# LSH attention before two feed-forward layers on one Trainium2 core: a pair's preparation takes all of the queries, then all of the keys

## Chip, cores and metric

One core of a Trainium2 chip runs the whole program. The metric is the device time of one execution in microseconds. A measurement is several executions; their median is compared.

## What is computed

For 2 batches of 8 heads, 768 positions and 64 dimensions, attention is masked by hash buckets: six sign bits of a projection give each query and each key a bucket, and only pairs in the same bucket count. Two feed-forward layers follow; they have no part in the change.

```python
q_bits = (np.einsum('bhsd,dk->bhsk', q, proj) > 0)
k_bits = (np.einsum('bhsd,dk->bhsk', k, proj) > 0)
mask = q_bucket[:, :, :, None] == k_bucket[:, :, None, :]
scores = np.where(mask, scale * q @ k.T, -1e9)
attn = softmax(scores)              # with + 1e-9 in the denominator
x = (attn @ v) as 1536 x 512
h = x @ w_in;  x = (h * cos(h)) @ w_out
out = (silu(x @ w_gate) * (x @ w_val)) @ w_out2
```

## The kernel before, in words

**Pairs and steps.** The 16 heads are taken as eight pairs. A pair is six steps of 128 query rows (steps 0 to 5; the code's `u` counts 48 of them, `i = u % 6`). `att_step` (L569) writes out the order of a step by hand: scores of head 0 (`mm_scores`, L421), transposes of the probabilities of two steps ago, the AV matmuls (`av`, L485) for a half pair finished before, scores of head 1, more transposes. VectorE takes the row maxima out of PSUM (L438), ScalarE the exponentials (L449), GpSimd multiplies by the reciprocal sums (the norms, L460, two to a step). Every engine works through its own queue in program order, and so does SP, which issues all transfers.

**Operands of the scores.** fp32 products are made of rounded high parts and low parts. For a pair of heads, `mm_scores` adds two matmuls in PSUM: X by Y (L429) and Z by W (L431). X holds the queries' high part in its first 64 rows and their low part in the others; Y holds the keys' high part twice; Z holds the queries' high part and, in 12 rows more, sign bits of the queries; W holds the keys' low part and sign bits of the keys. Each of the four has two buffers, so that one pair's are filled while the pair before is computed. The first scores of a pair (step 0) need all of the four.

**Preparation of a pair.** `prep(pr)` (L231) is a generator that is advanced at four places of every step (`fill`, L565), 24 times in a pair, while the pair before is computed. For pairs from 2 on it goes in this order:

- calls 1 and 3 (step 0): queries of head 0 and 1 are transposed on TensorE (L243), scaled and copied to `raw["q"]` (in the rows "qT") by ScalarE (L249);
- calls 5 and 7 (step 1): VectorE rounds the queries to `hi["q"]` ("qH", L257); the keys are transposed and copied to `raw["k"]` ("kT") by VectorE (L253);
- call 9 (step 2): VectorE rounds the keys ("kH"); SP is given eight copies of 192 KB, for each half X, Z, Y and Y (L260 to L263); TensorE projects (L285), VectorE makes the bits in a tile `bt` (L289), GpSimd scales them (L293), and SP is given eight transfers of bits, four to Z and four to W (L308);
- call 11 (step 2): GpSimd subtracts, `raw["q"] - hi["q"]`, in place (L314), and SP is given two transfers of it to X (L320);
- call 13 (step 3): the same for the keys, to W.

Since SP works in order and each transfer waits for its data, a transfer that waits holds all behind it. Pair 1 has the same parts with other places for bits and other counts of calls, within steps of pair 0; pair 0 is prepared by `prep_first` without transfers.

**What else SP issues.** Queries and keys of the pair after next are loaded at step 4 (`load_pair`, L213; "qn" and "kn"), values at step 5 ("vn"), and a weight block of 512 KB at steps 2 and 5 from u = 5 to u = 32 (`fetch_next`, L96, issues at L106 or L110). Three steps after its load a weight is rebuilt: one copy by ScalarE (L125) and three operations by VectorE (L140, L144, L148), spread over the fills of a step (steps 2 and 5 from u = 8 to u = 35).

**Small tiles.** The pool `sm` (L203) has eight buffers each of row minima (`mn`), sums (`sv`) and reciprocals (`rv`).

Of the kernel before, what the change touches and what calls it, by code (L numbers as in the profile page):

```python
# [10 lines left out]
F32 = mybir.dt.float32  # L11
# [3 lines left out]
ALU = mybir.AluOpType  # L15
PSUM = bass.MemoryType.PSUM

P = 128
# [8 lines left out]
def lsh_attention_moe_moe2(  # L27
# [13 lines left out]
    nc = tc.nc  # L41
# [158 lines left out]
    ld = actx.enter_context(tc.tile_pool(name="ld", bufs=1))  # L200
    pre = actx.enter_context(tc.tile_pool(name="pre", bufs=1))
    pp = actx.enter_context(tc.tile_pool(name="pp", bufs=6))
    sm = actx.enter_context(tc.tile_pool(name="sm", bufs=8))  # L203

    pj0 = {nm: pre.tile([P, D], F32, tag="pj0" + nm, name="pj0" + nm) for nm in "qk"}
    pjs = pre.tile([P, NB], F32, tag="pjs", name="pjs")
# [4 lines left out]
    heads = {}  # L211
# [15 lines left out]
    def prep_psum(pr, i, name):  # L227
        pool, tag = (ps_v, "av") if pr == 1 and i % 2 else (ps_p, "pp")
        return pool.tile([P, 512], F32, tag=tag, name=name)

    def prep(pr):  # L231
# [4 lines left out]
        X, Y, Z, W = (  # L236
            qk.tile([P, 2, S], F32R, tag=nm, bufs=2, name=f"{nm}{pr}") for nm in "XYZW"
        )
        for nm in ("q", "k"):
            for j in range(2):  # L240
                ps = prep_psum(pr, j, f"tr{nm}{pr}_{j}")
                for c in range(HB):
                    nc.tensor.transpose(  # L243
                        ps[:, c * P : (c + 1) * P],
                        nat[nm, pr][:, j, 2 * c : 2 * c + 2, :].rearrange("p c d -> p (c d)"),
                        ident,
                    )
                if nm == "q" or pr == 1:
                    nc.scalar.activation(  # L249
                        out=raw[nm][:, j, :], in_=ps[:, :HALF], func=AF.Copy, scale=TAKEN[nm]  # L250
                    )
                else:
                    nc.vector.tensor_copy(raw[nm][:, j, :], ps[:, :HALF])  # L253
                yield
                if pr > 1:
                    yield
            nc.vector.tensor_copy(hi[nm], raw[nm])  # L257
        for e in range(2):
            r, cs = slice(e * D, (e + 1) * D), slice(e * HALF, (e + 1) * HALF)
            nc.sync.dma_start(out=X[:D, :, cs].bitcast(F32), in_=hi["q"][r].bitcast(F32))  # L260
            nc.sync.dma_start(out=Z[:D, :, cs].bitcast(F32), in_=hi["q"][r].bitcast(F32))
            nc.sync.dma_start(out=Y[:D, :, cs].bitcast(F32), in_=hi["k"][r].bitcast(F32))
            nc.sync.dma_start(out=Y[D:, :, cs].bitcast(F32), in_=hi["k"][r].bitcast(F32))  # L263


        if pr == 1:
            bt = early.tile([P, 2, DM], F32, tag="raw", bufs=2, name="bt1")[:, :, :HALF]
            for j in range(2):
                ps = prep_psum(pr, j, f"pj1_{j}")
                for g, nm in enumerate(("q", "k")):  # L270
                    nc.tensor.matmul(
                        out=ps[g * D : (g + 1) * D, :HALF], lhsT=pj0[nm], rhs=raw[nm][:, j, :],
                        start=True, stop=True,
                    )
                nc.vector.tensor_scalar(
                    out=bt[:, j], in0=ps[:, :HALF], scalar1=0.0, scalar2=cvec[:, 1:2],
                    op0=ALU.is_gt, op1=ALU.subtract,
                )
        else:
            bt = pre.tile([P, HALF], F32, tag="bt", name=f"bt{pr}")  # L280
            ps = prep_psum(pr, 4, f"pj{pr}")
            for g, nm in enumerate(("q", "k")):
                for j in range(2):
                    r0 = 32 * (2 * g + j)
                    nc.tensor.matmul(  # L285
                        out=ps[r0 : r0 + 32, :HALF], lhsT=pj[nm], rhs=raw[nm][:, j, :],
                        start=True, stop=True,
                    )
            nc.vector.tensor_scalar(  # L289
                out=bt, in0=ps[:, :HALF], scalar1=0.0, scalar2=cvec[:, 0:1],  # L290
                op0=ALU.is_gt, op1=ALU.subtract,
            )
# [3 lines left out]
        for g, dst in enumerate((Z, W)):  # L296
            rows = slice(D, D + 2 * NB)
            for e in range(2):
                cs = slice(e * HALF, (e + 1) * HALF)
                if pr == 1:  # L300
                    r0 = D * g + 32 * e
                    nc.sync.dma_start(
                        out=dst[rows, :, cs].bitcast(F32), in_=bt[r0 : r0 + 2 * NB]
                    )
                    continue
                for j in range(2):
                    r0 = 32 * (2 * g + j) + 2 * NB * e
                    nc.sync.dma_start(  # L308
                        out=dst[rows, j, cs].bitcast(F32), in_=bt[r0 : r0 + 2 * NB]
                    )  # L310
        yield
        yield
        for nm in ("q", "k"):
            nc.gpsimd.tensor_tensor(  # L314
                out=raw[nm], in0=raw[nm], in1=hi[nm].bitcast(F32), op=ALU.subtract
            )
            for e in range(2):
                cs = slice(e * HALF, (e + 1) * HALF)
                dst = X[D:, :, cs] if nm == "q" else W[:D, :, cs]
                nc.sync.dma_start(out=dst.bitcast(F32), in_=raw[nm][e * D : (e + 1) * D])  # L320
            yield
            yield
        heads[pr] = (X, Y, Z, W)

    def prep_first():

# [20 lines left out]
                    )  # L347
            return ps

        def lows(eng, dst, j, nm, hi, e):  # L350
            r, cs = halves[e]
            eng.tensor_tensor(  # L352
                out=dst[:, j, cs], in0=raw[nm][r, j, :], in1=hi[:, j, cs].bitcast(F32),
                op=ALU.subtract,
            )

        ps = transposes(0)
        for j in range(2):
            for nm in ("q", "k"):
                nc.scalar.activation(  # L360
                    out=raw[nm][:, j, :], in_=ps[nm][:, :HALF], func=AF.Copy, scale=TAKEN[nm]
                )
            pb = ps_p.tile([P, 512], F32, tag="pp", name=f"pj0_{j}")
            for g, nm in enumerate(("q", "k")):
                nc.tensor.matmul(
                    out=pb[g * D : (g + 1) * D, :HALF], lhsT=pj0[nm], rhs=raw[nm][:, j, :],
                    start=True, stop=True,
                )
            if j == 0:
                ps = transposes(1)  # L370
            for dst, nm, es in ((Y, "k", (0, 1)), (X, "q", (0,))):
                for e in es:
                    r, cs = halves[e]
                    if j or nm == "k":
# [11 lines left out]
            lows(nc.gpsimd, W[:D], j, "k", Y[:D], 0)  # L386
            lows(nc.vector, X[D:], j, "q", X[:D], 0)
            nc.vector.tensor_scalar(
                out=bt[:, j, :], in0=pb[:, :HALF], scalar1=0.0, scalar2=cvec[:, 1:2],
                op0=ALU.is_gt, op1=ALU.subtract,  # L390
            )
            for e in range(2):
                cs = halves[e][1]
                src, dst = bt[D + 32 * e : D + 32 * e + 2 * NB, j], W[D : D + 2 * NB, j, cs]
                if e:
                    nc.gpsimd.tensor_scalar(
                        out=dst, in0=src, scalar1=-BIG, scalar2=1.0, op0=ALU.mult, op1=ALU.mult
                    )
                else:
                    nc.scalar.activation(out=dst, in_=src, func=AF.Copy, scale=-BIG)  # L400
            lows(nc.vector, W[:D], j, "k", Y[:D], 1)
            nc.vector.tensor_copy(Z[D : D + 2 * NB, j, :HALF], bt[: 2 * NB, j])
            yield
        for j in range(2):
# [7 lines left out]
            lows(nc.vector, X[D:], j, "q", X[:D], 1)  # L412
            yield

    scores = {}
# [469 lines left out]
```

## Time and profile before

| | |
|---|---|
| three runs | 819.39, 820.34, 823.87 us; median 820.34 |
| the profiled execution | 822.72 us, of which the span from the first to the last instruction is 820.9 |
| busy, share of the span | TensorE 97%, weight loads 76%, VectorE 57%, ScalarE 61%, GpSimd 55% |
| attention | from the start to about 265 us |
| feed-forward layers | from there to the end |
| issues on SP's queue, in the attention | copies of high parts, bits and low parts, loads of q, k, v, ten weight blocks |

How to read it: TensorE's busy time is modelled from pipelined matmuls, so a share near 100% says that it was fed, not that it was at its peak. What a stall is worth is read better from the distance between the same instructions of successive steps. The attention has a rhythm of six steps, and its stretches are compared with one another.

In the rows, PE is TensorE, PEld its weight loads, DVE VectorE, ACT ScalarE, POOL GpSimd, SPq the queue of SP.

### The profile page before, as it was taken

Reading aid. Unit: us, or ns where it says so; the run is one execution under the profiler, and the core shown is the slowest. Engines: PE = TensorE matmul, PEld = TensorE weight load, DVE = VectorE, ACT = ScalarE, POOL = GpSimd, SP = SyncE. Lnnn points to the kernel's source line nnn. Section 1 sums busy time; section 2 is a strip of 40 time slices with the busy share of each in tenths; the row PEclk is TensorE's granted clock in tenths of the full one; section 3 lists DMA queues with packets and bytes.
Section 4 is the critical chain, followed back from the end, with each engine's and each line's share of the span. In section 5 each row is a group of like instructions: output and inputs, shape, how many; then the busy total and the mean of one; then the engine's idle time right before and its main releaser. Section 6 shows DMA issues by size and latency. Waiting matters only on the chain.

```text
span 820.9 us, 11429 instructions
## 1 busy us (share of the span) xinstructions
PE 795.2 (97%) x3956; PEld 622.6 (76%) x3956; DVE 466.5 (57%) x865; ACT 499.6 (61%) x941; POOL 454.1 (55%) x394
## 2 busy tenths in 40 slices
PE   6899999998999999999999999999999999999998
PEld 4666666666675788888888888888888888888886
DVE  5888987887673999987755688752122111121112
ACT  5777767766685888887767777743334333343332
POOL 4754553653562677677776767744444444445440
PEclk8999999999999999999999999999999999999999
DMA  3745645644502455433220234300001000010001
GB/s 115 179 115 171 168 128 169 172 124 118 149 1 78 129 160 175 154 103 102 79 76 1 63 120 128 101 0 1 1 0 53 1 1 0 1 52 0 1 1 51
DMA packets 47049, 66.52 MB, mean 81 GB/s; under 512 B 3824, under 2 KB 41872, under 8 KB 46992
## 3 DMA queue, kind: packets, MB, share of 16 engines
q1 hardware_dynamic: 46992, 65.80, 27.4%
q8 instruction: 31, 0.51, 0.3%
q14 instruction: 26, 0.21, 0.1%
HBM read 45.09 MB, written 3.15 MB: 59 GB/s over the span
## 4 chain that ended last, share of the span: by engine, by line
PE 86%; DVE 6%; DMA 3%; issue 1%; POOL 1%; ACT 1%; SPq 1%; POOLq 0%; DVEq 0%; ACTq 0%
PE o L608 9%; PE o L610 9%; PE o L609 9%; PE av L491 6%; PE h L608 5%; PE h L610 5%; PE h L609 5%; PE t L473 5%; PE gate L609 4%; PE val L609 4%; PE val L608 4%; PE gate L608 4%; PE gate L610 4%; PE val L610 4%; PE s L429 3%; PE s L431 3%
## 5 line engine op out<-in xcount | busy, mean ns | idle before, releaser
L460 POOL TENSOR_SCALAR p<-p,rv 128x768 f32<-128x768 f32 x96 | 89.4, 942 | 106.3 <-DVE rv L457 99.2
L783 DVE TENSOR_TENSOR u<-val,sg 128x512 f32<-128x512 f32 x36 | 24.9, 692 | 198.7 <-ACT sg L777 188.4
L438 DVE TENSOR_SCALAR_CACHE_REDUCE p<-s 128x768 f32<-128x768 f32 x96 | 91.7, 955 | 46.7 <-PE s L431 38.4
L479 ACT ACTIVATE pt<-t 128x384 f32<-128x384 f32 x144 | 66.9, 486 | 53.6 <-PE t L473 53.5
L449 ACT ACTIVATE p<-p,mn 128x768 f32<-128x768 f32 x96 | 89.6, 934 | 9.4 <-DVE p L438 9.2
L473 PE MATMUL t<-ident,p 128*128 128x128 f32 x576 | 86.2, 274 | 6.0 <-DVE pt L481 5.6
L473 PEld LDWEIGHTS t<-ident,p 128*128 128x128 f32 x576 | 67.4, 140 | 17.1 <-DVE pt L481 7.5
L491 PE MATMUL av<-pt,vn 128*64 128x384 f32 x384 | 72.1, 498 | 0.0
L429 PE MATMUL s<-Y,X 128*128 128x512 f32 x192 | 59.2, 390 | 1.8 <-DVE X L352 1.8
L431 PE MATMUL s<-W,Z 76*128 76x512 f32 x192 | 51.2, 348 | 8.7 <-issue 3.8
L642 ACT ACTIVATE r<-r 128x512 f32<-128x512 f32 x48 | 30.4, 633 | 41.8 <-DVE r L634 41.8
L630 DVE SCALAR_TENSOR_TENSOR rf<-ki,h 128x512 f32<-128x512 int32 x46 | 32.0, 695 | 35.9 <-ACT ki L627 35.6
L429 PEld LDWEIGHTS s<-Y,X 128*128 128x128 f32 x192 | 29.3, 193 | 28.8 <-DVE pt L481 8.4
L125 ACT ACTIVATE w<-raw 128x512 f32<-128x512 f32 x68 | 44.6, 659 | 0.0
L491 PEld LDWEIGHTS av<-pt,vn 128*64 128x64 f32 x384 | 23.4, 136 | 25.8 <-issue 25.8
L654 DVE TENSOR_TENSOR g<-h,r 128x512 f32<-128x512 f32 x48 | 33.1, 689 | 16.9 <-ACT r L643 16.6
L431 PEld LDWEIGHTS s<-W,Z 76*128 76x128 f32 x192 | 30.3, 194 | 15.1 <-issue 7.9
L144 DVE SCALAR_TENSOR_TENSOR bw<-w,bw 128x512 int32<-128x512 int32 x55 | 38.0, 691 | 1.2
L140 DVE TENSOR_SCALAR bw<-raw 128x512 int32<-128x512 int32 x55 | 38.0, 691 | 1.0
L148 DVE SCALAR_TENSOR_TENSOR w<-raw,bw 128x512 int32<-128x512 int32 x55 | 37.5, 683 | 0.9
L643 ACT ACTIVATE r<-r,halfpi 128x512 f32<-128x512 f32 x48 | 34.8, 724 | 1.6
L627 ACT ACTIVATE ki<-h 128x512 int32<-128x512 f32 x48 | 28.3, 590 | 11.2 <-PE h L610 11.2
(1872 smaller groups left out, 2298.7 us busy)
## 6 DMA issues: line engine op xcount, KB each, us to landing
raw<-in_moe_w_out_dram SPq DMA_DIRECT2D x28, 512.0 KB
raw<-in_moe_w_in_dram SPq DMA_DIRECT2D x16, 512.0 KB
raw<-in_moe_w_gate_dram SPq DMA_DIRECT2D x12, 512.0 KB
raw<-in_moe_w_val_dram SPq DMA_DIRECT2D x12, 512.0 KB
Y<-kH SPq DMA_DIRECT2D x28, 192.0 KB
vn<-in_v_dram SPq DMA_DIRECT2D x8, 384.0 KB
out_dram<-ot SPq DMA_DIRECT2D x12, 256.0 KB
qn<-in_q_dram SPq DMA_DIRECT2D x7, 384.0 KB
```

The costliest lines, as they stand in the source:

```text
L125: nc.scalar.activation(out=t, in_=raws[i][:, :, 1].bitcast(F32), func=AF.Copy, scale=2.0**-112)
L429: nc.tensor.matmul(out=ps[:, ks], lhsT=X[:, j, qs], rhs=Y[:, j, ks], start=True, stop=False)
L431: nc.tensor.matmul(out=ps[:, ks], lhsT=Z[:KZ, j, qs], rhs=W[:KZ, j, ks], start=False, stop=True)
L438: nc.vector.tensor_scalar(out=pt, in0=ps[:, :S], scalar1=-MASKED, scalar2=None, op0=ALU.min, op1=ALU.min, accum_out=mn,)
L449: nc.scalar.activation(out=pt, in_=pt, func=AF.Exp, bias=nbias.pop((u, j)), scale=-1.0, accum_out=sums[u][:, j : j + 1],)
L460: nc.gpsimd.tensor_scalar(out=pt, in0=pt, scalar1=rv[:, j : j + 1], scalar2=1.0, op0=ALU.mult, op1=ALU.mult)
L473: nc.tensor.transpose(ps[:, c * P : (c + 1) * P], src[:, kb * P : (kb + 1) * P], ident)
L479: nc.scalar.activation(out=o, in_=s3, func=AF.Copy)
L491: nc.tensor.matmul(out=ps[j * D : (j + 1) * D, :HALF], lhsT=nat["v", pr][:, j, BLOCKS[kb], :], rhs=pts[half, j][:, kb, :], start=(kb == 0) ...
L608: nc.tensor.matmul(out=out_ap, lhsT=sh, rhs=mh, start=first, stop=False)
L609: nc.tensor.matmul(out=out_ap, lhsT=sh, rhs=ml, start=False, stop=False)
L610: nc.tensor.matmul(out=out_ap, lhsT=sl, rhs=mh, start=False, stop=last)
```

## The change

The preparation of a pair from 2 on takes all that belongs to the queries before the keys. X and Z are filled right after the queries are rounded (call 5), both halves of X, then both of Z; GpSimd makes the queries' low part in the same call and SP is given its two transfers. The low part goes to a tile of its own ("low"), since the transposed queries are still needed for the projection. After the projection the first half of the queries' tile takes the bits; the tile `bt` is gone. Y is filled in call 9, both halves of one copy, then of the other; bits and their transfers follow as before. The keys' low part comes in call 11, and the generator ends two calls earlier. For pair 1 only the order of the eight copies changes. `sm` has four buffers instead of eight. The helper of the same name in `prep_first` is renamed. The list `heads[pr]` is set at the beginning.

```diff
-    sm = actx.enter_context(tc.tile_pool(name="sm", bufs=8))
+    sm = actx.enter_context(tc.tile_pool(name="sm", bufs=4))
...
             nc.vector.tensor_copy(hi[nm], raw[nm])
-        for e in range(2):
-            r, cs = slice(e * D, (e + 1) * D), slice(e * HALF, (e + 1) * HALF)
-            nc.sync.dma_start(out=X[:D, :, cs].bitcast(F32), in_=hi["q"][r].bitcast(F32))
-            nc.sync.dma_start(out=Z[:D, :, cs].bitcast(F32), in_=hi["q"][r].bitcast(F32))
-            nc.sync.dma_start(out=Y[:D, :, cs].bitcast(F32), in_=hi["k"][r].bitcast(F32))
-            nc.sync.dma_start(out=Y[D:, :, cs].bitcast(F32), in_=hi["k"][r].bitcast(F32))
+            for dst in (X[:D], Z[:D]) if nm == "q" else (Y[:D], Y[D:]):
+                for e in range(2):
+                    r, cs = slice(e * D, (e + 1) * D), slice(e * HALF, (e + 1) * HALF)
+                    nc.sync.dma_start(
+                        out=dst[:, :, cs].bitcast(F32), in_=hi[nm][r].bitcast(F32)
+                    )
+            if pr > 1 and nm == "q":
+                lows(pr, nm, raw, hi)
...
-            bt = pre.tile([P, HALF], F32, tag="bt", name=f"bt{pr}")
...
+            bt = raw["q"][:, 0, :]
             nc.vector.tensor_scalar(
                 out=bt, in0=ps[:, :HALF], scalar1=0.0, scalar2=cvec[:, 0:1],
...
+        bits(pr, bt)
         yield
         yield
-        for nm in ("q", "k"):
-            nc.gpsimd.tensor_tensor(
-                out=raw[nm], in0=raw[nm], in1=hi[nm].bitcast(F32), op=ALU.subtract
-            )
...
+        for nm in ("q", "k") if pr == 1 else ("k",):
+            lows(pr, nm, raw, hi)
             yield
             yield
...
+    def lows(pr, nm, raw, hi):
+
+        X, _, _, W = heads[pr]
+        t = raw[nm]
+        if pr > 1 and nm == "q":
+            t = pre.tile([P, 2, HALF], F32, tag="low", name=f"{nm}L{pr}")
+        nc.gpsimd.tensor_tensor(out=t, in0=raw[nm], in1=hi[nm].bitcast(F32), op=ALU.subtract)
+        for e in range(2):
+            cs = slice(e * HALF, (e + 1) * HALF)
+            dst = X[D:, :, cs] if nm == "q" else W[:D, :, cs]
+            nc.sync.dma_start(out=dst.bitcast(F32), in_=t[e * D : (e + 1) * D])
```

`bits` is the block of eight transfers of L296 to L310 as a function, word for word.

## Rows read from the trace of the kernel before

**Rows 1.** Attention: length, busy PE, PEld, DVE, ACT, POOL, then PEclk, DMA share, GB/s.

```profile
20.00:265.00 245.00, 231.26 (x1481) 158.22 (x1482) 184.32 (x411) 175.01 (x383) 125.91 (x124) 1.00 0.49 132
```

**Rows 2.** The same view, from one step's first AV matmul to the next step's.

```profile
36.81:41.52 4.71, 4.71 (x33) 3.40 (x32) 2.97 (x8) 3.49 (x10) 1.79 (x2) 1.00 0.94 296
112.38:116.74 4.36, 4.36 (x29) 3.07 (x28) 4.08 (x7) 2.59 (x6) 4.31 (x4) 1.00 0.58 140
116.74:121.68 4.94, 4.60 (x30) 3.05 (x29) 4.30 (x10) 3.25 (x9) 2.33 (x4) 1.00 0.62 130
65.86:71.72 5.86, 5.14 (x32) 3.36 (x31) 5.39 (x14) 4.50 (x12) 1.96 (x2) 1.00 0.97 275
96.02:101.75 5.73, 5.15 (x33) 3.37 (x33) 5.29 (x13) 4.58 (x12) 1.95 (x2) 1.00 0.98 283
126.04:132.39 6.35, 4.93 (x32) 3.38 (x32) 5.18 (x11) 4.52 (x12) 1.96 (x2) 1.00 0.98 286
156.68:163.07 6.39, 5.15 (x33) 3.36 (x32) 5.60 (x14) 4.56 (x12) 2.02 (x3) 1.00 0.96 272
187.36:194.66 7.30, 4.92 (x33) 3.38 (x32) 5.18 (x11) 4.44 (x12) 1.96 (x2) 1.00 0.94 252
218.40:224.13 5.73, 4.60 (x30) 3.06 (x29) 2.63 (x8) 3.57 (x10) 1.78 (x2) 1.00 0.94 251
```

**Rows 3.** TensorE in order of time at two pair ends: start, duration, instruction, idle.

```profile
130.89 0.59 PE L431 MATMUL s<-W,Z 76*128 76x512 f32 x2 [1.42 <-issue]
...
162.27 0.55 PE L243 MATMUL trq<-ident,qn 128*128 128x128 f32 x3 [0.49 <-DMA qn<-in_q_dram]
```

**Rows 4.** The chain of work that ended last, at the end of pair 3.

```profile
125.26 4.58 DMA W<-kT
```

**Rows 5.** SP's queue in order of time, preparation of pair 4.

```profile
107.85 0.60 SPq L260 DMA_DIRECT2D X<-qH  x1
...
112.74 0.59 SPq L262 DMA_DIRECT2D Y<-kH  x1
...
114.68 0.73 SPq L261 DMA_DIRECT2D Z<-qH  x1
...
116.36 0.95 SPq L263 DMA_DIRECT2D Y<-kH  x1
117.41 3.23 SPq L308 DMA_DIRECT2D Z<-bt  x4
120.69 2.99 SPq L308 DMA_DIRECT2D W<-bt  x4
123.79 1.37 SPq L320 DMA_DIRECT2D X<-qT  x2
125.26 1.25 SPq L320 DMA_DIRECT2D W<-kT  x2
...
131.27 0.34 SPq L106 DMA_DIRECT2D raw<-in_moe_w_out_dram  x1
```

**Rows 6.** Busy time by engine, steps 2 to 4 of pair 3; DMA share and GB/s last.

```profile
114.00:120.00 6.00, 5.66 (x37) 4.04 (x38) 5.65 (x11) 3.09 (x7) 3.39 (x4) 1.00 0.90 202
120.00:125.00 5.00, 5.00 (x34) 3.65 (x34) 4.39 (x9) 4.24 (x12) 4.58 (x5) 1.00 0.10 22
```

**Rows 7.** GpSimd in order of time, steps 1 to 3 of pair 3.

```profile
107.41 2.03 POOL L460 TENSOR_SCALAR p<-p,rv 128x768 f32<-128x768 f32 x2 [3.42 <-DVE rv L457]
...
115.06 1.82 POOL L314 TENSOR_TENSOR qT<-qT,qH 128x768 f32<-128x768 f32 x1
...
121.25 1.83 POOL L314 TENSOR_TENSOR kT<-kT,kH 128x768 f32<-128x768 f32 x1
```

**Rows 8.** VectorE in order of time, step 2 of pair 3.

```profile
112.63 0.61 DVE L289 TENSOR_SCALAR bt<-pj,cvec 128x384 f32<-128x384 f32 x1
...
115.81 1.63 DVE L144 SCALAR_TENSOR_TENSOR w<-w,raw 128x512 int32<-128x512 int32 x1
117.47 0.69 DVE L148 SCALAR_TENSOR_TENSOR w<-raw,w 128x512 int32<-128x512 int32 x1
```

More of the change, by code (lines that the diff above doesn't have):

```diff
@@ L229, in prep_psum, with bits @@
         return pool.tile([P, 512], F32, tag=tag, name=name)
+    def bits(pr, bt):
+        _, _, Z, W = heads[pr]
+        rows = slice(D, D + 2 * NB)
+        for g, dst in enumerate((Z, W)):
+            for e in range(2):
+                cs = slice(e * HALF, (e + 1) * HALF)
+                if pr == 1:
+                    r0 = D * g + 32 * e
+                    nc.sync.dma_start(
+                        out=dst[rows, :, cs].bitcast(F32), in_=bt[r0 : r0 + 2 * NB]
+                    )
+                    continue
+                for j in range(2):
+                    r0 = 32 * (2 * g + j) + 2 * NB * e
+                    nc.sync.dma_start(
+                        out=dst[rows, j, cs].bitcast(F32), in_=bt[r0 : r0 + 2 * NB]
+                    )
     def prep(pr):
@@ L235, in prep @@
             hi[nm] = pre.tile([P, 2, HALF], F32R, tag=nm + "H", name=f"{nm}H{pr}")
-        X, Y, Z, W = (
+        X, Y, Z, W = heads[pr] = [
             qk.tile([P, 2, S], F32R, tag=nm, bufs=2, name=f"{nm}{pr}") for nm in "XYZW"
-        )
+        ]
         for nm in ("q", "k"):
@@ L257, in prep @@
             nc.vector.tensor_copy(hi[nm], raw[nm])
[L258 to L263 removed]
+            for dst in (X[:D], Z[:D]) if nm == "q" else (Y[:D], Y[D:]):
+                for e in range(2):
+                    r, cs = slice(e * D, (e + 1) * D), slice(e * HALF, (e + 1) * HALF)
+                    nc.sync.dma_start(
+                        out=dst[:, :, cs].bitcast(F32), in_=hi[nm][r].bitcast(F32)
+                    )
+            if pr > 1 and nm == "q":
+                lows(pr, nm, raw, hi)
         if pr == 1:
@@ L295, in prep @@
         )
[L296 to L310, printed above, removed]
+        bits(pr, bt)
         yield
         yield
-        for nm in ("q", "k"):
-            nc.gpsimd.tensor_tensor(
-                out=raw[nm], in0=raw[nm], in1=hi[nm].bitcast(F32), op=ALU.subtract
[L316 to L320, printed above, removed]
+        for nm in ("q", "k") if pr == 1 else ("k",):
+            lows(pr, nm, raw, hi)
             yield
             yield
-        heads[pr] = (X, Y, Z, W)
+    def lows(pr, nm, raw, hi):
[4 more added lines that the diff above has]
+        nc.gpsimd.tensor_tensor(out=t, in0=raw[nm], in1=hi[nm].bitcast(F32), op=ALU.subtract)
+        for e in range(2):
+            cs = slice(e * HALF, (e + 1) * HALF)
+            dst = X[D:, :, cs] if nm == "q" else W[:D, :, cs]
+            nc.sync.dma_start(out=dst.bitcast(F32), in_=t[e * D : (e + 1) * D])
     def prep_first():
@@ L348, in transposes, with rest_of @@
             return ps
-        def lows(eng, dst, j, nm, hi, e):
+        def rest_of(eng, dst, j, nm, hi, e):
             r, cs = halves[e]
@@ L385, in prep_first @@
             yield
-            lows(nc.gpsimd, W[:D], j, "k", Y[:D], 0)
-            lows(nc.vector, X[D:], j, "q", X[:D], 0)
+            rest_of(nc.gpsimd, W[:D], j, "k", Y[:D], 0)
+            rest_of(nc.vector, X[D:], j, "q", X[:D], 0)
             nc.vector.tensor_scalar(
@@ L400, in prep_first @@
                     nc.scalar.activation(out=dst, in_=src, func=AF.Copy, scale=-BIG)
-            lows(nc.vector, W[:D], j, "k", Y[:D], 1)
+            rest_of(nc.vector, W[:D], j, "k", Y[:D], 1)
             nc.vector.tensor_copy(Z[D : D + 2 * NB, j, :HALF], bt[: 2 * NB, j])
@@ L411, in prep_first @@
             )
-            lows(nc.vector, X[D:], j, "q", X[:D], 1)
+            rest_of(nc.vector, X[D:], j, "q", X[:D], 1)
             yield
```

## The prediction

> **What bounds the kernel now.** I read the stretches first: in the attention part TensorE is busy 231.26 of 245.00 us, so some 14 us are open there [rows 1]; in the two feed-forward parts behind it TensorE is not idle, and nothing of this change lies there. So the question is what TensorE waits for in the attention.
>
> Then I cut the attention at the starts of the AV matmuls, one such group to a step. A step without preparation work takes 4.36 us with TensorE busy throughout; a step that also has one of the four transposes of the next pair's preparation takes 4.71 [rows 2]. Against this stands the stretch over a pair's end, from the AV of step 5 to the AV of the next pair's step 0. With one query transpose in it, it should take 4.71, and does so from pair 0 to pair 1 (the 4.71 row is that one; it builds no weight). From pair 1 on it takes 5.86, 5.73, 6.35, 6.39, 7.30 and, where nothing is left to prepare, 5.73 against 4.36 [rows 2]. The excess is 1.15 + 1.02 + 1.64 + 1.68 + 2.59 + 1.37 = **9.45 us**.
>
> What is waited for: the first scores of the new pair. The matmul of W and Z starts at 130.89 after 1.42 us of idle, so it could have started at 129.47; at other pair ends the query transpose behind it waits for qn, the load of the pair after next, as at 162.27 [rows 3]. The profile puts the first wait down to "issue", but the chain of work names the real end: a transfer of kT to W that runs from 125.26 for 4.58 us [rows 4].
>
> Why is that transfer issued so late? GpSimd had the low part of the keys at 121.25 + 1.83 = 123.08 [rows 7], but the SP queue got to it at 125.26. SP issues one transfer after the other from 112.74 to 126.51: six of the eight copies of high parts (X and Z of the first half had gone out at 107.85), eight of sign bits (3.23 + 2.99 us), two of the queries' low part (1.37), two of the keys' (1.25), and only behind them qn [rows 5]. Meanwhile the DMA engines were nearly empty: 0.10 of their time from 120 to 125, against 0.90 at 202 GB/s before [rows 6]. At a pair's end the limit is the issue order on one queue.
>
> **The change, part by part.**
>
> Queries first. Of the 20 preparation transfers of a pair from 2 on, two (X and Z of the second half) now follow the first two at 107.85 instead of standing among those of the keys, and the two of the queries' low part follow as soon as GpSimd has made it. They take some 0.60 (as the X at 107.85), 0.73 and 1.37 us, so 2.70 with their gaps about 3.0 us of SP's time that leaves the crowded stretch [rows 5].
>
> When will those be issued? GpSimd does the low part right behind its two norms of step 1, which end at 107.41 + 2.03 = 109.44; with 1.82 for the subtraction it is ready at 111.27 [rows 7]. X, X, Z, Z go from 107.85 to about 110.5, the two low transfers from 111.3 to 112.7. One weight load that SP issued ahead of the queries (the kind at 131.27, 0.34 us) now stands behind them, since SP first waits for the queries of step 1. So Y's four start near 113.1 instead of 112.74: this gives back 0.4 us.
>
> Does SP then go faster? In the old burst the issues grew from 0.59 to 0.95 us [rows 5]. A copy of 192 KB at 202 GB/s is 0.97 us, by which I read 0.95 as SP paced by the engines. The new order puts more behind Y early on (six copies and a weight load), so I let Y take 0.60 to 0.95 each, 3.6 in all with gaps, and the bits 6.5 to 6.9 (they took 6.27 from the first to the end of the last). The keys' low part then goes out near 123.6, at best 122.2, at worst 124.4 (Y at 0.95 and the first group of bits drawn out likewise), instead of 125.26: 0.9 to 3.1 us earlier. I take 1.65. It gains again on arrival: the queries' 384 KB, at 202 GB/s 1.9 us, no longer stand ahead of it in the engines, of which I count 1.3. That makes about 3 us, estimates from the rows named, against losses of 1.02 to 2.59. The qn load moves with it, by 1.65 at least, and its waits were shorter than that. I expect the six stretches at 4.71 and 4.36 but for some 0.4 us at the largest and 0.15 us here and there: **gain 8.9 us**. The bounds are 0.9 per pair end, 6 x 0.9 = 5.4, and the whole 9.45.
>
> The Trainium skill, "DMA: Bandwidth & Descriptors", section Bandwidth, has copies within SBUF bound by the fabric at 435 GB/s; by that a 192 KB copy is 0.45 us (an estimate), SP would never be paced, and the gain were the full 9.45. The row's 202 GB/s with engines 0.90 busy decides for me.
>
> Low part of keys, two fill slots earlier. It takes the place on GpSimd that the queries' had, at 115.06, so DVE's weight step at 115.81 is held as before (1.63 us, [rows 8]) and the step after that keeps its 4.94 instead of 4.36 [rows 2]: no gain there. In step 3 GpSimd is freed of 1.83 us, which TensorE did not feel.
>
> A place of its own for the queries' low part: the same instruction with another output, 1.82 us; its old reader is a pair back. Nothing.
>
> Sign bits in the queries' tile: two new waits. VectorE writes the bits at 112.63 [rows 8] and must now find GpSimd done with that tile: 111.27, so 1.36 us to spare, with the row maxima queued behind it if that cover goes. ScalarE writes the next pair's queries there behind the next pair's first scores, later than 130.89 [rows 3], and must find the bits' transfers landed: these are issued by 124, and ScalarE's exponentials would queue behind. Both free.
>
> The weight load moved behind the queries is used three steps on, 13 us; free. Small tiles 8 to 4: rows are reused after two steps rather than four, after their readers; free (at worst one more semaphore look per step). Pair 1 only reorders its eight high copies; its pair end has no excess [rows 2].
>
> Sum: 822.72 in the profiled execution (span 820.9) less 8.9 is 813.8. That execution lies 2.4 above the median of the runs, so for the median 820.34 - 8.9 = **811.4**.
>
> **Rivals.**
>
> Half the gain (chance 0.25). Either SP stays paced throughout (0.9 per end: 814.9), or, freed of the wait, the pair end meets the next limit: five of the six also build a weight, and VectorE is busy about 5.2 to 5.6 us in them [rows 2], more than the 4.71. If each keeps the 0.58 of the step after 116.74, 2.9 us stay: 814.3. For it: VectorE's load. Against it: that 0.58 comes from a weight step held by GpSimd, and no low part lies at the pair's end.
>
> No gain (0.12): the wait is for bandwidth, not for issue. From 126 on the engines carry low parts, three loads and a weight load at 0.98 share [rows 2]; if W's last rows land with these whatever their issue, the time is 820. Or the change doesn't do what it says, because Y is held at SP behind the queries' low part by as much as was taken away. Against both: engines idle for five microseconds just before, and 111.27 + two issues is not later than the keys' high part.
>
> Slower (0.05): the queries' low part as a new gate. SP holds Y behind it, VectorE holds the bits and all row maxima behind it. If it ended 3 us late, at 114.3, Y would start at 115.6, the keys' low part be back at 125 to 126, and VectorE stand still from 112.63 to 114.3, 1.67 us in a step where it is busy 4.08 of 4.36 [rows 2]: 6 x 1.67 = 10.0, so 830. It costs nothing up to 1.36 us of delay. For it: the norms ahead of it took 2.03 us, [rows 7], not 1.79 as at the first pair's end [rows 2], drawn out while VectorE casts the queries. Against it: 0.24 us is all of that delay.
>
> The Trainium skill, "SBUF — State Buffer", section SBUF: two separate sides, says that GpSimd and certain VectorE instructions lock a shared port pair for a whole instruction. The 1.63 us at 115.81, against 0.69 for the like instruction behind it [rows 8], agrees; by that rule the low part in step 1 could hold, or be held by, VectorE for one instruction, which by these rows is under 2 us and no end of the range.
>
> **How the numbers follow.** Forecast 0.58, half 0.25, none 0.12, slower 0.05. The range 809 to 816 holds the first two with the scatter of the runs (a median may lie 2 us off); what is left out is no gain, slower and a little below. A measurement of this kernel can tell about 0.5%, 4.1 us: faster 0.83, same 0.12, slower 0.05.
>
> **What would show it.** Right: X and Z four in a row in step 1, the queries' low transfers before Y, the keys' low part issued at least 1 us earlier against the step; the six stretches at 4.4 to 5.1; no wait of W and Z matmuls at pair ends; the step after the build of step 2 still near 4.9. Wrong: a wait at pair ends of over 0.5 us on average; VectorE or SP waiting for GpSimd in steps 1 and 2; ScalarE waiting for transfers at its first query copy.

## The result, and the profile after

The changed kernel takes **813.37 us**, the median of four runs (812.93 to 813.44), where the kernel before took 822.11 beside it (four runs, 819.39 to 825.22): ratio 0.9891 [0.985, 0.9933]. The forecast of 811.4 against 820.34 was a ratio of 0.989. The two profiled executions differ a little more: 812.93 us with a span of 811.1, against 822.72 with 820.9, so 9.8 us of span are to be found.

The view of busy time from one step's AV to the next, of the kernel after (columns as in [rows 2]; first a pair end that builds no weight, then steps 2 and 3 of pair 3, then three of the six pair ends that had an excess; the three left out are 4.69 each):

```profile
35.92:40.63 4.71, 4.71 (x32) 3.39 (x32) 2.96 (x8) 3.49 (x10) 1.80 (x2) 1.00 0.93 300
109.66:114.02 4.36, 4.36 (x30) 3.07 (x29) 4.28 (x7) 2.65 (x6) 4.31 (x4) 1.00 1.02 257
114.02:119.07 5.05, 4.59 (x30) 3.05 (x29) 4.41 (x10) 3.13 (x9) 2.06 (x3) 1.00 0.81 142
65.24:69.93 4.69, 4.69 (x32) 3.39 (x31) 4.25 (x10) 3.98 (x11) 1.96 (x2) 1.00 0.96 306
...
123.43:128.12 4.69, 4.69 (x33) 3.40 (x32) 4.25 (x10) 3.98 (x11) 1.96 (x2) 1.00 0.94 300
...
210.02:214.38 4.36, 4.36 (x29) 3.07 (x28) 2.63 (x8) 3.15 (x8) 1.79 (x2) 1.00 0.66 207
```

All six pair ends are now as short as the undisturbed one: 5.86, 5.73, 6.35, 6.39, 7.30 and 5.73 [rows 2] have become 4.69 five times and 4.36. That is 37.36 - 27.81 = **9.55 us**. The row of 5.05 is the step behind the weight build of step 2, 4.94 before [rows 2]. The five such steps grew from 24.68 to 25.37 in all: 0.69 us lost. The start of the attention came 0.89 us earlier (first AV at 35.92 instead of 36.81), which is not the work of the change (last section). 9.55 - 0.69 + 0.89 = 9.75, the span's 9.8.

The groups of TensorE's instructions over the six pairs say the same. Kernel before, from the first AV shown in [rows 2] to the end of the last stretch (busy us, mean ns, then idle before them and its releasers):

```profile
L473 PE MATMUL t<-ident,p 128*128 128x128 f32 x445 | 67.3, 274 | 1.7 <-DVE pt L481 1.7
...
L431 PE MATMUL s<-W,Z 76*128 76x512 f32 (+1 forms) x148 | 38.6, 342 | 6.2 <-issue 3.8 <-DMA qn<-in_q_dram 2.4
L243 PE MATMUL trq<-ident,qn 128*128 128x128 f32 x36 | 6.1, 277 | 1.3 <-DMA qn<-in_q_dram 1.3
```

And after:

```profile
L487 PE MATMUL t<-ident,p 128*128 128x128 f32 x445 | 67.3, 274 | 2.4 <-DVE pt L495 2.4
...
L445 PE MATMUL s<-W,Z 76*128 76x512 f32 (+1 forms) x148 | 38.2, 339 | 0.0
L263 PE MATMUL trk<-ident,kn 128*128 128x128 f32 x36 | 5.9, 272 | 0.0
L263 PE MATMUL trq<-ident,qn 128*128 128x128 f32 x36 | 5.9, 272 | 0.0
```

The W and Z matmuls waited 6.2 us in all and the query transposes 1.3; now both wait for nothing. (The rest of the 9.55 was counted as TensorE being busy: 5.14 instead of 4.69, for instance, [rows 2].) Of the 7.5 us, the profile puts 3.7 down to qn, the load that SP issues right behind the keys' low part, though 2.4 of these stand before a matmul that reads W and Z. What idle is left, 2.4 us, stands before the transposes of p and is due to VectorE; before it was 1.7, so it grew by as much as the steps behind the weight builds.

SP's queue after, preparation of pair 4, answering to [rows 5]:

```profile
105.12 1.25 SPq L281 DMA_DIRECT2D X<-qH  x2
106.47 1.25 SPq L281 DMA_DIRECT2D Z<-qH  x2
108.54 1.24 SPq L337 DMA_DIRECT2D X<-qL  x2
109.83 0.59 SPq L106 DMA_DIRECT2D raw<-in_moe_w_out_dram  x1
110.52 2.80 SPq L281 DMA_DIRECT2D Y<-kH  x4
113.42 3.14 SPq L246 DMA_DIRECT2D Z<-qT  x4
116.61 4.02 SPq L246 DMA_DIRECT2D W<-qT  x4
120.73 1.38 SPq L337 DMA_DIRECT2D W<-kT  x2
```

X and Z go out four in a row, then the queries' low part, the weight load, and only then Y. The keys' low part is issued at 120.73, which is 2.70 us ahead of the AV at 123.43 that opens the pair end; before, at 125.26, it was 0.78 ahead of the one at 126.04 [rows 2, 5].

GpSimd's two low parts of that preparation:

```profile
106.69 1.83 POOL L333 TENSOR_TENSOR qL<-qT,qH 128x768 f32<-128x768 f32 x1
...
112.44 1.83 POOL L333 TENSOR_TENSOR kT<-kT,kH 128x768 f32<-128x768 f32 x1
```

and VectorE's sign bits and weight step:

```profile
110.00 0.61 DVE L312 TENSOR_SCALAR qT<-pj,cvec 128x384 f32<-128x384 f32 x1
...
112.99 1.84 DVE L144 SCALAR_TENSOR_TENSOR w<-w,raw 128x512 int32<-128x512 int32 x1
114.86 0.69 DVE L148 SCALAR_TENSOR_TENSOR w<-raw,w 128x512 int32<-128x512 int32 x1
```

The queries' low part is done at 106.69 + 1.83 = 108.52, so the bits at 110.00 find the tile free with 1.48 us to spare. The weight step of line 144 shares its time with the keys' low part, 112.44 to 114.27, and takes 1.84 us (1.63 before, [rows 8]), with the row maximum of the step queued behind it.

### The profile page after: what moved, and what is told of

It is laid out like the page before. It is cut to its first block, busy times and chain, and to the rows that moved or that the text cites. A ratio compares the mean times of both kernels' runs of the same rounds, so it can differ in the third digit from the quotient of the medians.

```text
span 811.1 us, 11431 instructions
## 1 busy us (share of the span) xinstructions
PE 792.4 (98%) x3956; PEld 621.9 (77%) x3956; DVE 462.5 (57%) x865; ACT 498.9 (61%) x941; POOL 455.8 (56%) x394
## 4 chain that ended last, share of the span: by engine, by line
PE 92%; DVE 6%; POOL 1%; issue 1%; ACT 0%; DMA 0%; SPq 0%; DVEq 0%; POOLq 0%
PE o L624 9%; PE o L622 9%; PE o L623 9%; PE av L505 8%; PE t L487 7%; PE h L622 5%; PE h L623 5%; PE h L624 5%; PE s L443 4%; PE val L624 4%; PE gate L624 4%; PE val L623 4%; PE gate L623 4%; PE val L622 4%; PE gate L622 4%; PE s L445 4%
```

## Experiments

The theory: at the pair ends TensorE waited for whatever SP issued last, and the change wins because the last transfers are issued earlier. Rivals: it is the queries' low part alone that matters; GpSimd's order of the low parts; the bytes; the smaller pool of small tiles.

### Each part of the change alone

**order**: the kernel before, in which only the copies of high parts are reordered; both low parts stay where they were.

```diff
-        for e in range(2):
-            ...
+            for dst in (X[:D], Z[:D]) if nm == "q" else (Y[:D], Y[D:]):
+                for e in range(2):
+                    r, cs = slice(e * D, (e + 1) * D), slice(e * HALF, (e + 1) * HALF)
+                    nc.sync.dma_start(
+                        out=dst[:, :, cs].bitcast(F32), in_=hi[nm][r].bitcast(F32)
+                    )
```

> The kernel before with one part of the change: X and Z of both halves are issued when the queries are rounded, Y when the keys are; the low parts stay where they were. Theory A (SP's issue order sets the wait at a pair's end): two issues, 0.60 + 0.73 us with gaps about 1.4, leave the burst ahead of the keys' low part, the queries' low part still stands ahead of it; W arrives some 1.2 us earlier, so of the losses 1.15, 1.02, 1.64, 1.68, 2.59, 1.37 about 0, 0, 0.4, 0.4, 1.4, 0.2 stay: some 7 us faster than before, ratio 0.991 to 0.994. Rival B (the wait is for DMA bandwidth near the pair's end, where nothing changes): within 1 us. Rival C (what counts is that GpSimd makes the keys' low part a step earlier): within 1 us, since GpSimd's order is that of before.

**lowq**: the kernel before with the other half alone: the queries' low part has its own tile, is made and sent right behind the queries' cast, the bits move to the queries' tile, and the small tiles' pool is at 4. The copies of high parts keep their old order, behind the keys' cast.

```diff
+            if pr > 1 and nm == "q":
+                low = pre.tile([P, 2, HALF], F32, tag="low", name=f"qL{pr}")
+                nc.gpsimd.tensor_tensor(
+                    out=low, in0=raw[nm], in1=hi[nm].bitcast(F32), op=ALU.subtract
+                )
+                for e in range(2):
+                    ...
+                    nc.sync.dma_start(
+                        out=X[D:, :, cs].bitcast(F32), in_=low[e * D : (e + 1) * D]
+                    )
         for e in range(2):
...
-            bt = pre.tile([P, HALF], F32, tag="bt", name=f"bt{pr}")
+            bt = raw["q"][:, 0, :]
...
-        for nm in ("q", "k"):
+        for nm in ("q", "k") if pr == 1 else ("k",):
```

> The kernel before with the other part: the queries' low part in step 1 and in a tile of its own, its two transfers issued there, bits in the queries' tile, four small tiles; X, Z and Y of the second half stay in the burst of the keys. Theory A: 1.4 us of issues leave the burst and 384 KB no longer stand ahead of W in the engines: W arrives about 2.7 us earlier, nearly all of 9.45 us comes back, ratio 0.989 to 0.991. Rival B: up to 6 us, through the bytes alone. Rival C: the full gain too (GpSimd's keys' low part comes a step earlier here), so this run doesn't tell A from C; the next one does.

**swap**: the kernel before; from pair 2 on the keys' low part is made and sent ahead of the queries'.

```diff
-        for nm in ("q", "k"):
+        for nm in ("q", "k") if pr == 1 else ("k", "q"):
```

> The kernel before with the low parts of keys and queries exchanged, on GpSimd and on SP: GpSimd makes the keys' low part in step 2, and W is issued before X. The number and the bytes of the transfers are those of before. Theory A: the last of the queue is now X, which the first score matmul needs 0.45 us before W; the wait moves from W and Z to Y and X and is as long or up to 0.45 us longer: 0 to 3 us slower, ratio 1.000 to 1.004. Rival C: W is there in time, and the gain is that of the changed kernel, ratio 0.99.

**after_again**: the changed kernel unaltered, beside these three.

> The changed kernel once more, as a reference for the other runs on the same chip: ratio 0.985 to 0.993. If the 0.9 us by which its first 36 us were shorter in its profile come from the chance of when TensorE's clock rises, its start may be longer or shorter by about a microsecond here, against an unchanged rest.

**sm4**: the kernel before with the small tiles' pool at 4.

```diff
-    sm = actx.enter_context(tc.tile_pool(name="sm", bufs=8))
+    sm = actx.enter_context(tc.tile_pool(name="sm", bufs=4))
```

> The kernel before with four buffers of small tiles instead of eight and nothing else. All theories: no difference, ratio 0.996 to 1.004; were it faster, the pool would be a cause of its own.

Measured:

```
kernel        us (lowest to highest)      ratio to before, 95% interval
order         813.33 (813.04 - 813.59)    0.9880 [0.9859, 0.9902]
lowq          835.86 (833.35 - 839.36)    1.0157 [1.0122, 1.0192]
swap          820.62 (818.99 - 823.71)    0.9974 [0.9954, 0.9995]
after_again   813.30 (812.85 - 813.94)    0.9878 [0.9852, 0.9904]
sm4           821.29 (819.34 - 827.87)    0.9997 [0.9971, 1.0024]
```

The order of the high copies alone gives the whole gain, more than I had expected of it; the queries' low part alone costs 13 us where I had expected a gain; the pool is worth nothing; exchanging the low parts makes it faster by 0.3%, where I had expected up to 0.4% slower. So the rival of GpSimd's order falls: in order the keys' low part is made where it was, and the gain is there; in swap it is made a step earlier, and the gain is not. SP's queue of **order**, preparation of pair 4:

```profile
105.20 1.25 SPq L261 DMA_DIRECT2D X<-qH  x2
106.55 1.25 SPq L261 DMA_DIRECT2D Z<-qH  x2
107.85 0.66 SPq L106 DMA_DIRECT2D raw<-in_moe_w_out_dram  x1
110.19 2.54 SPq L261 DMA_DIRECT2D Y<-kH  x4
...
119.12 1.37 SPq L320 DMA_DIRECT2D X<-qT  x2
120.59 1.25 SPq L320 DMA_DIRECT2D W<-kT  x2
```

Both low parts are still the last two of the queue, as before, and yet the keys' goes out at 120.59, earlier than in the changed kernel (120.73). What counted was to begin the rest early: with X and Z gone by 107.80, only Y's four copies are left to send when the keys' cast is done. They take 2.64 us up to the first bits (110.19 to 112.83), where six took 4.67 (112.74 to 117.41, [rows 5]). Two copies fewer save 2.03 us, not the 1.4 that I had counted, since the last copies of the longer row were the slow ones.

SP's queue of **lowq**, preparation of pair 3, shows the loss:

```profile
84.72 1.25 SPq L265 DMA_DIRECT2D X<-qL  x2
86.48 0.34 SPq L106 DMA_DIRECT2D raw<-in_moe_w_out_dram  x1
86.93 0.61 SPq L270 DMA_DIRECT2D X<-qH  x1
87.65 0.97 SPq L271 DMA_DIRECT2D Z<-qH  x1
...
100.81 1.37 SPq L330 DMA_DIRECT2D W<-kT  x2
```

In the kernel before, X and Z of the first half need the queries' cast alone, and nothing that waits stood ahead of them in SP's queue: SP had run ahead and issued them in step 1, at 107.85 for pair 4 [rows 5]. In lowq SP first waits for GpSimd's low part, then comes the weight load of the next step, and all eight high copies follow in the crowded stretch, which lasts from 86.93 to 100.81, 13.9 us, against 12.5 from 112.74 to 125.26 [rows 5]. The two transfers that left it were replaced by two that were pushed in, and what is sent last got later.

**lowq_head** puts that to the test: lowq, with X and Z of the first half sent ahead of the low part.

```diff
             if pr > 1 and nm == "q":
+                for dst in (X, Z):
+                    nc.sync.dma_start(
+                        out=dst[:D, :, :HALF].bitcast(F32), in_=hi["q"][:D].bitcast(F32)
+                    )
...
+            if pr == 1 or e:
                 nc.sync.dma_start(out=X[:D, :, cs].bitcast(F32), ...)
                 nc.sync.dma_start(out=Z[:D, :, cs].bitcast(F32), ...)
```

> The run with the queries' low part alone, with one thing given back: X and Z of the first half are issued ahead of the queries' low part in step 1, as SP did of itself in the kernel before, where it ran ahead. X and Z of the second half stay in the burst. Theory A, as the other runs have it (what counts is when the last transfer of the pair is issued, and in the run without this the two copies lost their head start, so that eight copies stood in the burst behind a weight load): the keys' low part goes out 1 to 2.5 us earlier against the step than in the kernel before, the waits fall from 1.5 to 4.4 us to 0 to 0.5 us, time 813 to 816. Rival E (an early low part does harm by itself, through GpSimd or through a transfer that lands between others): still slower than the kernel before, above 825.

Measured: 816.23 us (814.68 to 817.64), ratio 0.9929 [0.9902, 0.9955]. Two transfers in another place turn 1.0157 into 0.9929: the lost head start was lowq's loss. It came out a little worse than I expected: the keys' low part goes out 0 to 1.4 us earlier than in the kernel before, not 1 to 2.5 (table below), and one wait of over 1 us stays. It also says what the queries' low part is worth by itself, some 5 to 6 us, as long as the head start stays. Two pair ends of lowq_head, with the smallest (0.06 us) and the largest (1.29) of the waits that are left:

```profile
124.05:128.80 4.75, 4.75 (x32) 3.38 (x32) 4.31 (x10) 4.04 (x11) 1.96 (x2) 1.00 0.95 289
...
182.88:188.86 5.98, 5.00 (x32) 3.36 (x32) 5.25 (x11) 4.49 (x12) 1.96 (x2) 1.00 0.78 228
```

### The last transfer delayed, without bytes

**delay2** and **delay4**: the changed kernel, with two or four more transfers of 12 x 16 bytes into a spare tile behind the sign bits: SP's time is spent, and next to no bytes are moved.

```diff
         bits(pr, bt)
+        if pr > 1:
+            spare = pre.tile([P, 4, 4], F32, tag="spare", name=f"spare{pr}")
+            for n in range(2):
+                nc.sync.dma_start(out=spare[: 2 * NB, n], in_=bt[: 2 * NB, :4])
```

> The changed kernel with two transfers of 12 rows by 16 bytes more on SP's queue between the bits and the keys' low part, which move next to nothing and hold SP for about 1.5 us. Theory A: the keys' low part leaves 1.5 us later; with an estimated 0.7 to 1.0 us to spare in the changed kernel the wait at six pair ends comes back with 0.5 to 0.8 us each: 3 to 5 us slower than the changed kernel. Rival B (bandwidth): no difference.

> As before with four such transfers, about 3 us of SP. Theory A: 2.0 to 2.3 us of wait at each of six pair ends, 12 to 14 us slower than the changed kernel, 1.5 us more per end than with two: the time is again that of the kernel before or above it. Rival B: no difference.

Measured: delay2 817.02 (814.41 to 819.95), ratio 0.9948 [0.9922, 0.9973], 3.7 us above the changed kernel; delay4 829.24, ratio 1.0102 [1.0066, 1.0138], 15.9 above it, a little more than expected. That is the median of three executions; a fourth, the profiled one, took 2034 us (last section) and says nothing of the waits, so the same kernel was run once more:

> The changed kernel with four small transfers more, once more, for a profile: the keys' low part goes out about 3 us later against the step than in the changed kernel, between 0 and 1.3 us behind the first AV matmul of step 5, and each of the six pair ends waits 2 to 3.5 us; time 827 to 831.

Measured: 832.2 us, ratio 1.0117 [1.005, 1.0185]; the waits came out wider than expected, 0.7 to 4.2 us (table below). SP's queue of **delay2**, preparation of pair 4:

```profile
118.65 2.99 SPq L246 DMA_DIRECT2D W<-qT  x4
121.68 1.47 SPq L323 DMA_DIRECT2D spare<-qT  x2
123.26 1.37 SPq L341 DMA_DIRECT2D W<-kT  x2
```

and the pair end that follows, in delay2:

```profile
125.01:130.52 5.51, 5.00 (x32) 3.36 (x31) 5.07 (x11) 4.52 (x12) 1.95 (x2) 1.00 0.94 275
```

Two transfers of 192 bytes take 1.47 us of SP, and a wait of 5.51 - 4.69 = 0.82 us is back. Next to no bytes were added, so the wait came back through the time of issue alone. In one table, from the traces: by how much the last transfers of a pair's set (those of the keys' low part; in swap X, the queries') are issued after the AV of step 5 (minus: ahead of it), and the wait that follows, that is the stretch less 4.69, at the last less 4.36, for the six pair ends from 1 to 2 on (after_again and after_c are two further profiles of the changed kernel):

```
              issued, us after the AV                    wait, us
after       -2.93 -2.43 -2.70 -2.89 -2.13 -3.23   0    0    0    0    0    0
after_again -2.91 -1.64 -1.40 -1.92 -2.51 -3.14   0    0.01 0.28 0    0.02 0
after_c     -3.06 -2.51 -2.82 -1.84 -1.90 -2.96   0    0    0.33 0    0    0
order       -2.82 -2.65 -2.90 -2.19 -2.85 -1.73   0    0    0    0.34 0.02 0
lowq_head   -1.85 -1.28 -1.44 -0.97 -0.42 -1.31   0    0.26 0.06 0.59 1.29 0
delay2      -0.89 -1.44 -1.75 -0.76 -0.62 -1.57   0.78 0.18 0.82 0.92 0.90 0
before      -0.81 -0.82 -0.78 -0.32 -0.40 +0.08   1.17 1.04 1.66 1.70 2.61 1.37
sm4         -0.80 -0.81 -0.80 -0.77 -0.35 -0.15   0.62 1.27 0.99 0.87 3.80 1.16
swap        -0.72 -0.01 -0.83 -0.82 -0.47 -0.11   0.72 1.74 1.56 0.93 3.39 0.58
delay4_b    +0.14 +0.47 +0.77 +1.98 -0.19 -0.06   3.96 1.87 3.06 4.16 2.23 0.72
lowq        +0.65 +1.21 +1.23 +0.67 +1.33 +0.58   4.38 3.69 3.72 2.14 3.48 1.49
```

Issued 2 us or more ahead, the transfers leave at most 0.34 us of wait; one to two ahead, 0 to 0.8; half a microsecond to one ahead, 0.6 to 1.7 in most cases; at the AV or behind it, up to 4.4.

Not all of the wait is in this one number: -0.80 gives 0.62 as well as 0.99. Two more things show in the traces. The first is qn, which SP issues right behind the last low part and which the query transpose of the pair end needs. swap sends the keys' low part 1.5 to 2.3 us ahead, and the profile names X as what TensorE then waits for at two pair ends (0.26 and 2.07 us), but qn, before the query transpose, at five (0.06 to 1.35). One of them, in **swap**, TensorE in order of time:

```profile
131.03 0.55 PE L243 MATMUL trq<-ident,qn 128*128 128x128 f32 x3 [1.35 <-DMA qn<-in_q_dram]
```

The waits that are left in order (0.34), after_again (0.28) and after_c (0.33) stand before that transpose too. The chain of work that ended last, in **after_c** at the end of pair 3, where the keys' low part went out 2.82 us ahead:

```profile
122.58 5.51 DMA qn<-in_q_dram
```

So it is the whole end of SP's queue that has to leave early, the last low part and qn behind it. At the last of the six ends, where there is no qn, the low part alone made the wait of 1.37 in the kernel before.

The second is TensorE's clock: in the two longest waits of sm4 and swap (3.80 and 3.39) the granted clock of the stretch is 0.87 and 0.88, so a part of the time is slower work. In **sm4**:

```profile
185.28:193.77 8.49, 6.01 (x32) 4.29 (x31) 5.61 (x14) 4.88 (x13) 2.22 (x3) 0.87 0.78 223
```

What sets the time from issue to landing (4.58 us for W [rows 4], 5.51 here) was not tested: no run changes the bytes.

### The step that got longer

**klate**: the changed kernel, with the keys' low part made one step later, where GpSimd made it before the change.

```diff
         bits(pr, bt)
         yield
         yield
+        if pr > 1:
+            yield
+            yield
         for nm in ("q", "k") if pr == 1 else ("k",):
```

> The changed kernel with the keys' low part back in step 3 (two fill slots later, as in the kernel before). Theory A with the port rule: SP reaches the keys' low part only after the bits, so nothing is lost there (GpSimd has it about 120.5 on the clock of the changed kernel's profile, SP at 120.7); VectorE's weight step L144 of step 2 is no longer held and the five steps behind it go from 5.03 to 5.22 us back towards 4.36: 2 to 3.5 us faster than the changed kernel, ratio to before about 0.986. Rival C (GpSimd's earlier keys' low part makes the gain): the losses at the pairs' ends come back, ratio near 1. Rival D: the held steps cost TensorE nothing and the reciprocal in step 4 is held instead: within 1 us of the changed kernel.

It was run again beside the changed kernel, **klate_b** and **after_c**:

> The changed kernel with the keys' low part in step 3 once more, on one chip with the changed kernel: 2 to 3.5 us below it, 810 to 811.5, all steps behind a weight step at 4.36 to 4.4 us.

> The changed kernel, as the reference beside the run before: 812.8 to 814.

Measured: klate 810.66 us, 0.988 [0.9856, 0.9905]; klate_b 810.55 (809.93 to 811.8), 0.9859 [0.981, 0.9909]; after_c, beside klate_b, 813.34 (812.78 to 813.75), 0.9888 [0.9846, 0.9929]. So this version beats the changed kernel by 2.8 us, with no run of the one reaching the other, and the kernel before by 10.6. The step behind the build of step 2 in **klate_b**, for pairs 1 and 4:

```profile
55.98:60.36 4.38, 4.38 (x31) 3.07 (x30) 3.38 (x9) 3.21 (x9) 2.67 (x3) 1.00 1.00 198
...
141.24:145.62 4.38, 4.38 (x30) 3.07 (x29) 3.39 (x9) 3.22 (x9) 2.65 (x3) 1.00 0.90 167
```

Why: VectorE's weight step of line 144 in the attention, ten times, by its line's view (shortest, median, longest in ns). In the changed kernel:

```profile
L144 DVE SCALAR_TENSOR_TENSOR w<-w,raw x10: 686/1254/2008, 54.6 to 185.0; 128x512 int32<-128x512 int32 x10
```

and in klate_b:

```profile
L144 DVE SCALAR_TENSOR_TENSOR w<-w,raw x10: 685/687/689, 54.9 to 181.8; 128x512 int32<-128x512 int32 x10
```

GpSimd's subtraction had lain beside five of these ten (1821 to 2008 ns; the other five take 686, and the median of 1254 lies between the two groups). Moved to where VectorE has no weight step, it takes the same 1.82 us:

```profile
116.30 1.82 POOL L336 TENSOR_TENSOR kT<-kT,kH 128x768 f32<-128x768 f32 x1
```

The Trainium skill, "SBUF — State Buffer", section SBUF: two separate sides, says that a VectorE instruction with two inputs in SBUF and a GpSimd instruction that reads SBUF hold a shared port pair for a whole instruction, one after the other. The 1821 to 2008 ns beside the subtraction, against 686 without it, agree with it. Now a small VectorE instruction on the sums (L473) is drawn out beside it, 0.53 us where it took 0.16 in the changed kernel, and TensorE loses nothing by it: the step in which it lies takes 4.36. On SP nothing is lost either: in klate_b the low part is ready at 118.12 and SP comes to it at 119.52.

## Why the prediction was right, and where its terms were off

**The cause: right.** The wait was for the last issue on SP. It went with the earlier issue, and came back with two small transfers (delay2). The rival of no gain falls with the same runs. How much the load of the DMA engines adds to the time from issue to landing, and so to how early is early enough, stays open. I had named W as what is waited for and qn's waits as shorter; qn is the other half of the queue's end, and what is left in three of the later profiles waits for it. Half the gain falls too: with the wait gone VectorE is busy 4.25 of 4.69 us at the pair ends that I feared (5.2 to 5.6 in the old, longer stretches), and TensorE waits for nothing there.

**The size: right, by 0.65 us** (9.55 against 8.9 at the pair ends). Y starts 0.86 us after the AV of step 2 (110.52, 109.66), where I had 0.72 (113.1, 112.38). Its four copies took 2.80 against 3.6. The bits took 7.2 us (113.42 to 120.63) against 6.5 to 6.9. The keys' low part came 1.92 us earlier against the pair end's AV, against 1.65. Over the six ends it came 1.6 to 3.3 us earlier, and in this profile nothing of the 0.4 us that I kept at the largest stayed; in the two other profiles of the changed kernel 0.28 and 0.33 did, at one end each. The 1.3 us that I counted on arrival, for the queries' 384 KB no longer ahead in the engines, no run shows: in order these bytes still go ahead of the keys', and its ends lose 0.36 us in all. The bits found 1.48 us to spare, against 1.36.

**The Trainium skill's rate**, from "DMA: Bandwidth & Descriptors", section Bandwidth, would have given the full 9.45, which is what came. Its reason is not borne out: from 112.30 to 118.30 the engines of the changed kernel were 0.95 busy at 210 GB/s, under half of 435. The gain is full since the last transfers leave 2.1 to 3.2 us ahead of the AV.

```profile
112.30:118.30 6.00, 5.54 (x36) 3.92 (x35) 5.67 (x11) 3.94 (x10) 3.40 (x4) 1.00 0.95 210
118.30:121.00 2.70, 2.70 (x19) 1.53 (x18) 1.67 (x5) 2.70 (x7) 1.33 (x3) 1.00 0.10 18
```

The second row shows the same 0.10 as [rows 6]: the engines are idle again while SP hands out sign bits, only now nothing waits for it.

**What made it: wrong.** I had put both moves into one sum: X and Z of the second half, and the queries' low part, together 3.0 us of SP. The runs show that each alone is enough or nearly so: order 0.988, lowq_head 0.9929. They do not add, since beyond some 2 us of lead there is little more to win. The forecast came out although its split was wrong, and that much of it is luck. And the second move alone, without the head start, loses: lowq, 1.0157. That X and Z of the first half are issued at 107.85 [rows 5] I had read as a fact about two transfers, not as SP's having run ahead to a point where nothing blocked it.

**The slower rival's mechanism exists.** SP did stand behind the queries' low part, and it cost 13 us in lowq. In the change it does not decide, as X and Z go ahead of it. My price for it (830, against 835.86) was near by luck: I had it from VectorE standing still, and lowq loses its time at the pair ends. My condition, a low part 3 us late, was wrong too: in lowq it is not late at all; it only stands ahead of copies that could have gone. One of my signs of being wrong did show: SP waits for GpSimd in step 1, from 107.72 to 108.54. It costs little, as the keys' cast ends only at 110.08 and Y starts at 110.52.

**The step behind the build: mis-sized.** "The step after that keeps its 4.94": it became 5.03 to 5.22, 0.69 us in all lost. I moved the keys' low part into the place of the queries' and called it even; it starts a little later against line 144 (0.55 us ahead of it instead of 0.75), so it holds it longer. The larger miss is that I took this hold as given: klate takes it away for 2.8 us.

**Free, as said**: the small tiles' pool (sm4, 0.9997) and ScalarE's wait for the bits' transfers, of which there is no trace. The weight load and the tile of its own were not tried alone.

**The absolute number** lies 2.0 us off, 813.37 against 811.4. Nearly all of that is the base, 822.11 in these runs against 820.34.

## What to carry to other kernels

When an engine waits for a transfer while the DMA engines are idle, list the issuing queue in order of time and move what is ready early ahead of the first instruction that waits; a transfer put ahead of others that are ready, but waiting itself, takes their head start away and can cost more than it wins. Measure the lead of the last transfer against its reader: once there is enough of it, further moves win nothing. Put GpSimd's operations on two SBUF tensors where VectorE has none such, and look for VectorE instructions that take two lengths. Look at what else stands at the end of the queue: a load behind the last transfer can be the next wait.

## What the runs showed of the hardware that I had not expected

**A transfer of 192 bytes costs SP as much as one of 192 KB.** Two of 12 x 16 bytes took 1.47 us of SP's queue in delay2, the two of the keys' low part behind them 1.37.

**A long wait costs twice.** In lowq TensorE stands nearly still at a pair end, and behind that, when it works again, the granted clock falls. Busy time by engine in lowq, the pair end at 99.60 (PEclk is the third figure from the end):

```profile
103.00:104.00 1.00, 0.02 (x1) 0.00 (x0) 0.96 (x4) 1.00 (x3) 0.00 (x0) 1.00 1.01 243
104.00:105.00 1.00, 0.28 (x1) 0.30 (x2) 0.43 (x1) 0.17 (x2) 0.00 (x0) 1.00 0.84 226
...
106.00:107.00 1.00, 0.50 (x3) 0.50 (x4) 0.65 (x4) 0.17 (x1) 0.12 (x1) 0.60 1.06 393
107.00:108.00 1.00, 1.00 (x7) 0.67 (x6) 0.00 (x0) 0.56 (x2) 1.00 (x2) 0.50 1.02 339
```

0.50 is 1.2 of 2.4 GHz. In the pair ends of the kernel before the granted clock stayed at 1.00 [rows 2]; in lowq the steps behind four of the six pair ends are longer too (5.29 to 6.08 us, where such a step takes 5.01), so the waits are not its whole loss.

**The start differs from one execution to the next, and with it the rise of the clock.** The first AV shown lay between 35.86 and 36.81 us in thirteen profiles of these kernels (all but delay4's), and in three of the changed kernel itself at 35.92, 36.54 and 36.45. Kernel before, early in the span:

```profile
18.00:20.00 2.00, 2.00 (x11) 1.90 (x10) 1.67 (x5) 1.33 (x5) 0.26 (x1) 0.50 0.00 0
```

and after:

```profile
18.00:20.00 2.00, 2.00 (x14) 1.60 (x14) 1.60 (x6) 1.71 (x5) 0.20 (x1) 0.91 0.00 0
```

The profile of before happens to have the latest first AV, that of after nearly the earliest: 0.89 us of the 9.8, where the other two profiles of the changed kernel would have given 0.27 and 0.36. That the clock makes all of this is not shown: klate's clock had risen by 20 us and fell to 0.50 again from 26 to 32, and its first AV came at 36.80.

**One execution of delay4 took 2034 us**, with TensorE's transposes at 535 ns instead of 274 and its AV matmuls at 1115 instead of 498, about twice as long. Its trace holds no record of the granted clock, so the 1.00 that its views print says nothing; five other executions of that kernel lay between 826.94 and 833.5. No run explains it.
